# Linear attention and GEGLU block: projections, token products, later outputs and down as 64-row streams of two tiles

## The chip, the cores and the metric

The kernel runs on one core of a Trainium2 chip. The metric is the device time of one execution in microseconds (us), as a median of several runs. Inside the core, TensorE (PE) multiplies matrices into the eight banks of PSUM, each matmul with a weight load of its own (PEld); VectorE (DVE) and ScalarE (ACT) read PSUM and write SBUF; GpSimd (POOL) works on SBUF; SyncE (SP) issues most DMA transfers, plain and transposing ones, from one queue in order.

## The reference

2048 tokens of 448 features go through a layer norm, linear attention with 16 heads of 28 features, a residual, a second layer norm, a gated MLP of width 1792 and a second residual, in bfloat16.

```python
qkv = (layernorm(x) @ wqkv)            # q, k, v: 16 heads of 28
phi = lambda t: jnp.where(t > 0, t + 1, jnp.exp(t)) + 1e-6
pq, pk = phi(q), phi(k)
kv = einsum("bhsd,bhse->bhde", pk, v)
z  = einsum("bhsd->bhd", pk)
num = einsum("bhqd,bhde->bhqe", pq, kv)
den = einsum("bhqd,bhd->bhq", pq, z)[..., None] + 1e-6
h  = x + (num / den) @ wo
y  = layernorm(h)
out = h + (gelu(y @ w_gate) * (y @ w_up)) @ w_down
```

## The kernel before

The 2048 tokens are 16 tiles of 128. The program is a graph of named tasks, each on one engine; each engine runs its tasks in an order written out by hand (`ORDERS`, numbers of tasks), and waits on semaphores for what it reads. `HOLD` says of some tasks which of several waits comes first. So nothing is scheduled when it runs: an engine that waits holds back all that stands behind.

**First part, per tile.** Loads (`dx`, `dwqk`), statistics (`bnst`, `bnag`, L398, L399), logarithm and exponential for the inverse deviation on ScalarE (L405, L407), normalization on VectorE for tiles 0 to 3 (`normD`, L420) and on GpSimd for the others (`normP`, L438). The normalized tile is transposed by TensorE for tiles 0 to 3 (`tr`, L428) and by DMA for the others (`xT`, L440). Features then are the rows: 448 of them are chunks of 128, 128, 128 and 64 rows, with the last padded by zeros, so the projections to K (`k_t`) and Q (`q_t`) are four matmuls of 128 rows and 448 columns a tile (L454). ScalarE and VectorE make the positive features: for K `ek`, `ck`, `pk` (L465 to L467), for Q `eq`, `rq` (L481, L482) and later `cq`, `aq` (L533, L534). The token product (`pt`, L473) adds up normalized x times K's features over all tiles in PSUM banks 4 to 7, four matmuls a tile; chunk 3 has a row block of ones, which gives z.

**Middle.** `z1`, `z0` (L499, L500) spread z, `evp` evicts the product, `kv` (L512) multiplies it by V's weights, `kvm` (L516) masks it by heads, and `w2` (L521) folds in wo: four groups of 112 rows.

**Per pair of tiles (`a2_pair`).** `cq`, `aq`, the product with z on GpSimd (`t1`, L538), its sum per head (`dr`, L541), inverse (`rd`), the scaled features (`pn`, L545), their transposition (`tro` on TensorE for pair 0, a DMA `oT` for the others), the output (`out`, L573, four matmuls of 112 rows a tile), the residual (`hr`, L579), second statistics, normalization (`nh`), a copy `wrap` that doubles the 448 features so that gate can read them in lanes 0 to 63 and up in lanes 64 to 127, and the transposition into hnT (`trh` on TensorE for tiles 0 and 1, DMAs `hT` for the others).

**MLP.** Chunks of 2, 2, 4, 4 and 4 tiles. A group `gu` computes gate (L653) and up (L655) alternately as two 64-row streams, seven pairs for each 128 hidden features; `ge` (L673) is gelu, `hm` (L675) the product, each in two halves of 256 columns. Then `down` (L625), 14 matmuls of 128 rows a tile; `fo` (L629) adds the residual and `do` stores. w_down is loaded by `dwd`.

The decoded order of TensorE from the last projections on reads:

```
... k_14 pt1_10 pt1_11 k_15 pt1_12 q_5 pt1_13 pt1_14 pt3_10 pt1_15 pt3_11 pt3_12 pt3_13 pt3_14 pt3_15
q_7 q_6 kv q_8 w2_1 w2_3 w2_0 q_9 tro_0 w2_2 q_11 out1_0 tro_1 q_10 out1_1 q_12 q_15 q_14 out2_2
trh_0 trh_1 q_13 gu2_0 gu2_1 out2_4 gu2_2 ... gu2_9 down448_0 gu2_11 gu2_10 out2_8 down448_1 ...
```

SP's queue ends its first part with twelve `xT`, then `dwg0 dwu0 dwg1 dwu1 oT_1 oT_2 oT_3 hT_2 hT_3 dwd oT_4 ...`.

Of the kernel before, what the change touches and what calls it, by code (L numbers as in the profile page):

```python
# [740 lines left out]
```

## Time and profile before

| | |
|---|---|
| median of three runs | 193.62 us (193.48 to 193.82) |
| profiled execution, first to last instruction | 192.1 us |
| matmuls | 1572 |
| first gate/up matmul | 51.19 us from the start |
| last matmul ends | 189.7 us |
| VectorE, ScalarE, GpSimd busy | 131.0, 77.9, 50.7 us |

Times in the profile count from the first instruction. A busy time of TensorE overlaps from matmul to matmul, because the next starts before the last has left the array; what a matmul costs in a stream is therefore read from the distance of starts and not from its duration. `PE ps L454 x4` in the chain of work means four matmuls of line 454 one behind the other; "SPq" is SyncE's queue, "PEld" the weight load. A "slot" below is the distance from one matmul's start to the next one's in a full stream.

### The profile page before, as it was taken

How to read it: one execution, taken by the hardware profiler on the slowest of the kernel's cores; microseconds unless marked ns; L12 is line 12 of the kernel's file. 1: busy time of each engine (PE TensorE's matmuls, PEld its weight loads, DVE VectorE, ACT ScalarE, POOL GpSimd, SP SyncE). 2: the span in 40 equal slices, each digit the busy share in tenths (PEclk: the TensorE clock that was granted, in tenths of full speed). 3: DMA queues.
4: the chain of work that ended last, by engine and by line, in shares of the span. 5: the costliest groups of instructions: out<-in, count | busy, mean ns of one | idle time of the engine just before them, and what ended most of it. 6: DMA issues, size and time to landing. Idle time of an engine off the chain costs nothing.

```text
span 192.1 us, 4004 instructions
## 1 busy us (share of the span) xinstructions
PE 187.2 (97%) x1572; PEld 105.4 (55%) x1572; DVE 131.0 (68%) x355; ACT 77.9 (41%) x226; POOL 50.7 (26%) x92
## 2 busy tenths in 40 slices
PE   7989999999999999999999999999999999999995
PEld 7444455555778776564445545544555545455454
DVE  2899978999999998979967446736544542244412
ACT  3697745599954342043044420024444420044200
POOL 7068630560263287404190000450000000000000
PEclk9999999999999999999999999999999999999999
DMA  6976557998205977520082134307700001010011
GB/s 185 379 183 82 113 102 168 220 214 133 55 3 102 184 227 130 119 54 5 0 82 42 37 53 93 89 9 86 182 0 3 0 3 43 4 48 3 0 48 48
DMA packets 35330, 16.96 MB, mean 88 GB/s; under 512 B 27696, under 2 KB 34032, under 8 KB 35312
## 3 DMA queue, kind: packets, MB, share of 16 engines
q1 hardware_dynamic: 35168, 16.60, 41.0%
q8 instruction: 12, 0.20, 0.5%
q10 hardware_dynamic: 144, 0.11, 0.3%
q14 instruction: 6, 0.05, 0.1%
HBM read 8.26 MB, written 1.84 MB: 53 GB/s over the span
## 4 chain that ended last, share of the span: by engine, by line
PE 82%; DMA 7%; ACT 6%; DVE 3%; POOL 1%; issue 0%; SPq 0%; POOLq 0%
PE ps L653 38%; PE ps L625 22%; PE ps L454 9%; PE ps L473 6%; PE ps L573 5%; DMA wd_sb<-in_B_w_down_dram 4%; DMA x_sb<-in_A_x_dram 2%; ACT pq L482 1%; ACT eq L481 1%; DVE st L398 1%; PE ps L655 1%; DVE hh L675 1%; ACT ln L405 1%; ACT e L465 1%; DVE x_sb L579 1%; PE ps L521 0%
## 5 line engine op out<-in xcount | busy, mean ns | idle before, releaser
L653 PE MATMUL ps<-hnT,wgu_sb 64*128 64x512 bf16 (+1 forms) x490 | 86.2, 333 | 0.1
L655 PE MATMUL ps<-hnT,wgu_sb 64*128 64x512 bf16 (+1 forms) x490 | 86.3, 333 | 0.0
L673 ACT ACTIVATE gl<-ps 128x256 bf16<-128x256 f32 x112 | 37.0, 380 | 83.1 <-PE ps L653 83.0
L653 PEld LDWEIGHTS ps<-hnT,wgu_sb 64*128 64x128 bf16 x490 | 45.4, 94 | 34.5 <-issue 2.2
L675 DVE TENSOR_TENSOR hh<-ps,gl 128x256 bf16<-128x256 f32 x112 | 42.8, 417 | 30.7 <-ACT gl L673 30.6
L655 PEld LDWEIGHTS ps<-hnT,wgu_sb 64*128 64x128 bf16 x490 | 45.2, 94 | 1.2
L625 PE MATMUL ps<-wd_sb,hh 128*128 128x448 bf16 (+1 forms) x238 | 43.6, 342 | 0.2 <-DMA wd_sb<-in_B_w_down_dram 0.2
L625 PEld LDWEIGHTS ps<-wd_sb,hh 128*128 128x128 bf16 x238 | 23.0, 98 | 20.2 <-issue 0.8
L454 PE MATMUL ps<-wqk_sb,xnT 128*128 128x448 bf16 x128 | 27.9, 352 | 0.7 <-ACT xnT L433 0.6
L538 POOL TENSOR_TENSOR t<-pq,zbc 128x448 f32<-128x448 bf16 x15 | 16.6, 1117 | 38.7 <-DVE pq L534 21.9
L629 DVE TENSOR_TENSOR x_sb<-ps,x_sb 128x448 bf16<-128x448 f32 (+1 forms) x17 | 10.0, 591 | 18.3 <-PE ps L625 18.3
L398 DVE BATCH_NORM_STATS2 st<-x_sb 128x6 f32<-128x448 bf16 x32 | 19.2, 611 | 4.0 <-DMA x_sb<-in_A_x_dram 4.0
L454 PEld LDWEIGHTS ps<-wqk_sb,xnT 128*128 128x128 bf16 x128 | 12.0, 98 | 12.0 <-ACT xnT L433 0.9
L473 PE MATMUL ps<-pk,xnn 128*128 128x448 bf16 x64 | 14.1, 353 | 0.0
L573 PE MATMUL ps<-w,pqnT 112*128 112x448 bf16 x64 | 13.6, 353 | 0.0
L579 DVE TENSOR_TENSOR x_sb<-ps,x_sb 128x448 bf16<-128x448 f32 x16 | 9.7, 613 | 2.8 <-PE ps L573 2.8
L465 ACT ACTIVATE e<-ps 128x448 bf16<-128x448 f32 x16 | 8.5, 540 | 5.7 <-PE ps L454 5.7
L402 POOL TENSOR_SCALAR nm<-mv 128x1 f32<-128x1 f32 (+1 forms) x19 | 4.1, 223 | 25.2 <-DVE mv L399 24.7
L608 POOL TENSOR_SCALAR hn<-x_sb,nm,rs 128x448 bf16<-128x448 bf16 x14 | 10.5, 754 | 0.8
L545 DVE TENSOR_TENSOR pqn<-pq,rd 128x448 bf16<-128x448 bf16 x16 | 9.9, 640 | 0.0
L467 DVE SCALAR_TENSOR_TENSOR pk<-ps,e 128x448 bf16<-128x448 f32 x16 | 9.7, 614 | 0.2
L541 DVE TENSOR_REDUCE den<-t 128x16 f32<-128x448 f32 x16 | 9.7, 604 | 0.0
(65 smaller groups left out, 125.4 us busy)
## 6 DMA issues: line engine op xcount, KB each, us to landing
out_dram<-x_sb SPq DMA_DIRECT2D x15, 112.0 KB, 1.8
wd_sb<-in_B_w_down_dram SPq DMA_DIRECT2D x1, 1568.0 KB, 7.8
x_sb<-in_A_x_dram SPq DMA_DIRECT2D x3, 448.0 KB, 6.0
wgu_sb<-in_B_w_gate_dram SPq DMA_DIRECT2D x1, 896.0 KB, 12.4
wgu_sb<-in_B_w_up_dram SPq DMA_DIRECT2D x1, 896.0 KB, 16.4
wqk_sb<-in_A_wqkv_dram SPq DMA_DIRECT2D x1, 672.0 KB, 4.9
wgu_sb<-in_B_w_gate_dram SPq DMA_DIRECT2D x1, 672.0 KB, 6.2
wgu_sb<-in_B_w_up_dram SPq DMA_DIRECT2D x1, 672.0 KB, 8.7
```

What stands on the lines that cost most here:

```text
L398: op("dve", lambda e: e.bn_stats(st[:, t, :], src_ap), [b_src], [b_st[t]], "bnst%s_%d" % (tag, t))
L454: ins = e.matmul(ps[:, bk, 0:D], xnT[:, t, k, :], wqk_sb[:, k, c0:c0 + D], start=(k == 0), stop=(k == 3))
L473: ins = e.matmul(ps[:, BK_PT[c], 0:D], xnn[:, t % XN_R, c * 128:(c + 1) * 128], pk[:, ip, :], start=(t == 0), stop=(t == T - 1))
L538: op(eng, lambda e, t=t, n=n: e.tensor_tensor(t1[:, n, :], pq[:, t, :], zbc[:, :], ALU.mult), [b_pq[t]] + b_z, [b_t1[n]], "t1%s_%d" % (eng ...
L573: ins = e.matmul(ps[:, BK_OUT[n], 0:D], pqnT[0:GW, i2, n, g, :], w2[:, g, :], start=(g == 0), stop=(g == NG - 1))
L579: op("dve", lambda e, t=t, bo=bo: e.tensor_tensor(x_sb[:, t, :], ps[:, bo, 0:D], x_sb[:, t, :], ALU.add), [b_ps[bo], b_x[t]], [b_x[t]], "h ...
L608: op("pool", lambda e, t=t, sh=sh: e.tensor_scalar(hn[:, sh, 0:D], x_sb[:, t, :], nm2[:, t:t + 1], rs2[:, t:t + 1], ALU.add, ALU.mult), [b ...
L625: ins = e.matmul(psO, hh[:, j, (t % HR) * 128:(t % HR + 1) * 128], wd_sb[:, j, c0:c1], start=(j == 0), stop=(j == NJ - 1))
L653: first = e.matmul(psG[:, jj * N:(jj + 1) * N], wgu_sb[A_, k, j * 128:(j + 1) * 128], hnT[A_, ka_, c0:c0 + N], start=(k == 0), stop=(k == ...
L655: ins = e.matmul(psU[:, jj * N:(jj + 1) * N], wgu_sb[B_, k, j * 128:(j + 1) * 128], hnT[B_, kb_, c0:c0 + N], start=(k == 0), stop=(k == NK ...
L673: G.add("act", lambda e, gi=gi, cs_=cs_, psG=psG: e.activation(gl[:, gi, cs_], psG[:, cs_], AF.Gelu_apprx_tanh), r=[b_ps[BK_G[i]]], w=[b_g ...
L675: op("dve", lambda e, dst=dst, srcU=srcU, srcL=srcL: e.tensor_tensor(dst, srcU, srcL, ALU.mult), [b_ps[BK_U[i]], b_glh], [b_ar[j_][t % HR] ...
```

## The change

Two tiles are worked on together wherever TensorE can hold them as two 64-row streams, one in lanes 0 to 63 and one in lanes 64 to 127, which write different PSUM banks. Each result then takes two passes, `a` and `b`, that swap the lanes; the second pass waits on a semaphore until the first has ended (`sync`).

- Projections (`proj1`, `proj2`): tiles 0 and 1 keep four 128-row matmuls each; all other K and Q go by pairs. Pass a has chunks 0 to 2, pass b chunks 0 to 3, and in chunk 3 each tile uses its 64 rows of features alone, for which the last 64 rows of weights are loaded into both halves (`wqka`, `wqkb`).

```diff
+        def proj2(what):
+            bk0 = slot(2)
+            prev = []
+            for part, chunks in (("a", (0, 1, 2)), ("b", (0, 1, 2, 3))):
+                def fproj(e, W, part=part, chunks=chunks):
+                    ins = None
+                    for c in chunks:
+                        for i_, (kind, t) in enumerate(what):
+                            h = t % 2 if part == "b" else 1 - t % 2
+                            W(2 * c + i_)
+                            c0 = D if kind == "K" else 0
+                            ins = e.matmul(ps[:, bk0 + i_, 0:D], xnT[HALF[h], t, c, :], wqk_sb[HALF[h], c, c0:c0 + D], start=(part == "a" and c == 0), stop=(c == 3))
+                    return ins
...
+                prev = [G.add("pe", fproj, r=reads, w=[(b_ps[bk0 + i_], i_) for i_ in range(2)], name="".join("%s%d" % w for w in what) + part, mw=True, sync=prev)]
```

- Token products (`pt_pair`) run by pairs of tiles in passes of two chunks; `w2` is made by two passes of 64 and 48 rows.
- Normalized x (`xnn`) lies by pairs, an odd tile's last 64 features behind the even tile's; the odd tile needs a second small normalization (`normT`) on GpSimd. The DMA transposes of tiles 6 to 15 take a pair each (`XT_GROUPS`); xnT now lies in the space of hh.
- w2 is copied by eight small DMAs (`dw2_0` to `dw2_7`, `pack_w2`) into w2p, 448 features over 128-row chunks; pairs 2 to 7 multiply by it with 3 + 4 slots, pair 1 by w2 in rows of 64 and 48, pair 0 as before by tiles:

```diff
+                    if p < P_PACK:
+                        prog = [(g, n, KH[(s + n) % 2][0], w2) for g in range(NG) for n in range(2)]
+                    else:
+                        prog = [(g, n, HALF[(s + n + 1) % 2], w2p) for g in range(3 + s) for n in range(2)]
...
+                            ins = e.matmul(ps[:, BK_OUT[n], 0:D], pqnT[rows, i2, n, g, :], w[rows, g, :], start=(g == 0 and s == 0), stop=(g == 3 and s == 1))
```

- Down of tiles 0 to 13 runs by pairs; tiles 14 and 15 stay as they were. The residual and the store take a pair:

```diff
+        def b2_pair(a):
+            prev = []
+            for s in range(2):
+                def fnd(e, W, s=s):
+                    ins = None
+                    for j in range(NJ):
+                        for n in range(2):
+                            t, h = a + n, (s + n) % 2
+                            W(2 * j + n)
+                            ins = e.matmul(ps[:, BK_O[n], 0:D], hh[HALF[h], j, (t % HR) * 128:(t % HR + 1) * 128], wd_sb[HALF[h], j, :],
+                                           start=(s == 0 and j == 0), stop=(s == 1 and j == NJ - 1))
+                    return ins
...
+            op("dve", lambda e: e.tensor_tensor(x_sb[:, a:a + 2, :], ps[:, BK_O[0]:BK_O[1] + 1, 0:D], x_sb[:, a:a + 2, :], ALU.add),
```

- The steps `ek`, `ck`, `pk`, `eq`, `rq`, `cq`, `aq`, `dr`, `rd`, `pn`, `hr` and most `wrap` take two tiles (896 columns) in one instruction, except for tiles 0, 1, 14 and 15 where noted by `K_SINGLE` and pair 0. `ge` and `hm` take 512 columns in one instruction in the first three chunks (`WIDE = (0, 1, 2)`).
- Transposes on TensorE become 64 rows wide, two at a time, with each half evicted by another engine (`evxA`/`evxD`, `evoA`/`evoD`, `evhA`/`evhD`). For tiles 0 and 1 the copy of the normalized features is computed by GpSimd (`dupP`). `pn` of pairs 2 and later leaves a small copy on GpSimd (`pd`). The DMA transposes hT of tiles 4 and up take a pair each.
- x tiles 2 and 3 are loaded ahead of the K and Q weights:

```diff
+    LOADS = "sp:x0 act:x1 sp:x2-3 sp:wqk sp:wqka sp:wqkb sp:x4-7 sp:x8-11 sp:x12-15"
+    SEQ = "K0 Q0 K1 Q1 K2K3 Q2Q3 K4K5 K6K7 K8K9 K10K11 K12K13 K14K15 Q4Q5 Q6Q7 Q8Q9 Q10Q11 Q12Q13 Q14Q15"
```

- All orders are new. TensorE's, decoded (`pt31_2` is the pass of chunks 3 and 0, second kind, from tile 2):

```
warm tr_0 tr_1 tr_2 K0 tr_3 Q0 Q1 K1 K2K3a K2K3b pt10_0 pt10_1 Q2Q3a pt30_0 Q2Q3b pt30_1 pt11_0
pt11_1 pt31_0 K4K5a pt31_1 K4K5b pt31_2 pt11_2 pt30_2 K6K7a pt10_2 K6K7b ... K14K15a pt31_8 K14K15b
pt11_8 ... pt30_14 pt30_15 pt11_12 pt11_14 pt11_15 Q4Q5a pt10_14 pt10_15 Q4Q5b Q6Q7a kv Q6Q7b
w2a_0 w2a_2 w2b_0 Q8Q9a w2b_2 Q8Q9b tro_0 Q10Q11a tro_1 Q10Q11b out1_1 Q12Q13a out1_0 Q12Q13b
Q14Q15a trh_1 Q14Q15b outa_1 trh_0 outb_1 gu2_0 ... gu2_6 downa_0 outa_2 downb_0 outb_2 gu2_7 gu2_8
outa_3 gu2_9 outb_3 gu2_10 gu2_11 outa_4 gu2_12 gu2_13 downa_2 outb_4 downb_2 gu4_15 gu4_14 outa_5
gu4_17 gu4_16 outb_5 ... gu4_55 gu4_54 downa_12 down448_14 downb_12 down224_15 down224_15
```

VectorE's, from kvm on:

```
kvm pn1_0 dr2_2 evwD_1 pn1_1 evwD_3 evoD_0 rd2_2 cq_4 evoD_1 aq_4 pn2_2 hr1_1 bnst2_1 bnag2_1 hr1_0
nhD_1 bnst2_0 bnag2_0 dr2_4 evhD_1 nhD_0 cq_8 cq_6 aq_8 evhD_0 cq_10 aq_6 hr2_2 bnst2_3 hm0_0 dr2_6
hm0_1 bnst2_2 rd2_4 bnag2_3 hm0_2 pn2_4 hm0_3 cq_12 bnag2_2 aq_12 hm0_4 dr2_8 rd2_6 hm0_5 wrap1_2
aq_10 wrap1_3 hm0_6 ...
```

SP's: `dx0 dx2 dwqk dwqka dwqkb dx4 dx8 dx12 dwv dwv_t dwo`, seven `xT`, `dwg0 dwu0 dwg1 dwu1`, `dw2_0` to `dw2_7`, `oT_1 dwd oT_2 hT_2 hT_3 oT_3 oT_4 hT_4 hT_6 do_0 ...`.

More of the change, by code (lines that the diff above doesn't have):

```diff
@@ L77, in __init__, with add @@
         self.order = None
-    def add(self, eng, fn, r=(), w=(), name="", kind="op", after=(), mw=False, cost=(), half=()):
+    def add(self, eng, fn, r=(), w=(), name="", kind="op", after=(), mw=False, cost=(), half=(), sync=()):
         t = _Task()
@@ L96, in dep @@
             t.dep_at[d.idx] = min(t.dep_at.get(d.idx, k), k)
+        for d in sync:
+            t.deps.append(d)
+            d.ncons += 1
+            t.dep_at[d.idx] = 0
+            t.full.add(d.idx)
         r = [x if isinstance(x, tuple) else (x, 0) for x in r]
@@ new lines, in bass_sequential_preLN__linear_attn_block__glu_gated_geglu__prompt_kernel, with slot, proj1, fproj @@
+        b_xt = bufs("xt", T)
+        slots, projs = [0], []
+        def slot(n):
+            s = slots[0]
+            slots[0] = (s + n) % 4
+            return s
+        def proj1(kind, t):
+            bk = slot(1)
+            c0 = D if kind == "K" else 0
+            def fproj(e, W):
+                ins = None
+                for c in range(4):
+                    W(c)
+                    ins = e.matmul(ps[:, bk, 0:D], xnT[:, t, c, :], wqk_sb[:, c, c0:c0 + D], start=(c == 0), stop=(c == 3))
+                return ins
+            projs.append(G.add("pe", fproj, r=b_xnT[t] + [b_w[kind][0], (b_w[kind][1], 3), (b_w[kind][2], 3)], w=[b_ps[bk]], name="%s%d" % (kind, t), mw=True))
+            if kind == "K":
+                k_act(t, 1, bk)
+            else:
+                q_post(t, 1, bk)
```

486 lines of the change are left out of this document (316 added, 170 removed), and 75 rows, old and new, of tables (HOLD, ORDERS).

## The prediction

> **What bounds the kernel now.** I read the page first (busy shares, slices, the chain that ended last), then the times of stretches, then the waits, then the shapes.
>
> ```profile
> span 192.1 us, 4004 instructions
> PE 187.2 (97%) x1572; PEld 105.4 (55%) x1572; DVE 131.0 (68%) x355; ACT 77.9 (41%) x226; POOL 50.7 (26%) x92
> PEclk9999999999999999999999999999999999999999
> PE 82%; DMA 7%; ACT 6%; DVE 3%; POOL 1%; issue 0%; SPq 0%; POOLq 0%
> ```
>
> The profiled execution has 192.1 us, the median of the three runs is 193.62; the 1.5 us between them lie outside the span and I carry them over unchanged. TensorE is full, at full clock. So the first question is how many matmul slots the change takes away, the second whether the other engines let TensorE use the gap. The stretches answer where they might not (columns: length, then PE, PEld, DVE, ACT, POOL busy):
>
> ```profile
> 11.02:37.36 26.34, 26.22 (x137) 13.25 (x138) 24.04 (x68) 16.78 (x50) 13.01 (x27) 1.00 0.68 131
> 37.36:51.19 13.83, 13.70 (x100) 7.66 (x98) 13.41 (x35) 13.30 (x35) 4.90 (x5) 1.00 0.76 137
> 51.19:64.00 12.81, 12.81 (x188) 10.00 (x190) 12.51 (x37) 6.96 (x18) 5.36 (x9) 1.00 0.47 72
> 132.00:179.00 47.00, 47.00 (x393) 23.38 (x390) 20.89 (x54) 15.75 (x48) 0.00 (x0) 1.00 0.18 36
> ```
>
> Until the first gate/up group at 51.19 us VectorE is nearly as full as TensorE (13.41 of 13.83), and ScalarE too (13.30). After some 90 us only TensorE is. A slot saved late is therefore time saved; a slot saved before 51.19 counts only if VectorE's list gets shorter as well.
>
> **The price of a slot.** From the chain and from the rows of the gate/up line between 125.8 and 156.1 us:
>
> ```profile
> 26.77 3.03 PE ps L454 x16
> 50.30 0.82 ACT hnT L604
> 51.12 0.07 issue
> 51.19 0.27 PE ps L653
> 112.03 1.62 PE ps L573 x8
> 118.95 1.52 PE ps L573 x8
> 120.47 5.30 PE ps L625 x28
> 125.77 0.32 PE ps L653
> 126.09 0.21 PE ps L653
> L653 PE MATMUL ps<-hnT,wgu_sb x140: 376/376/387, 125.7 to 155.7; 64*128 64x512 bf16 x140
> L625 PE MATMUL ps<-wd_sb,hh 128*128 128x448 bf16 x210 | 40.9, 353 | 0.2 <-DMA wd_sb<-in_B_w_down_dram 0.2
> ```
>
> A 128-row matmul of 448 columns takes 3.03/16 = 0.189 us, in the down line too (5.30/28). The gate/up matmuls are 64-row streams already: 140 pairs start within 30.0 us, 30.0/139 = 0.216 us for 512 columns of both halves. That is 0.189 × 512/448: a pair of 64-row streams costs what one 128-row matmul of the same width costs. So packing for its own sake (token products, down) is worth nothing; only dropped slots count. Changing between the two forms costs time: the same eight output matmuls take 1.62 us when they come behind 64-row work and 1.52 behind 128-row work, and the first gate/up matmul behind the down line takes 0.32 instead of 0.21: 0.10 us each way.
>
> **Part by part.**
>
> *K and Q.* 448 features are 3.5 chunks of 128; before, each tile pays 4 slots. Two tiles as 64-row streams pay 3 + 4 = 7 instead of 8. Fourteen pairs: 14 × 0.189 = 2.65 us fewer, all before the gate/up groups.
>
> *Later outputs.* With w2 packed by 128 rows, pairs 2 to 7 pay 7 slots instead of 8: 6 × 0.189 = 1.13 us, all after 51.19. Pairs 0 and 1 keep 8.
>
> *Token products and down:* 64 and 196 slots as before: 0. If the pairs of 448 columns differed from 0.189 by 1 ns, the 412 slots that become such streams would move 0.4 us; I keep ±0.4.
>
> *Changes of form.* From the first gate/up group on there are 15 now (each run of L573 or L625 between gate/up groups costs two); in the new order down and outputs have the form of the groups around them, and 3 are left, at the last down tiles. 12 × 0.10 = 1.2 us saved. Before that group there is 1 now; the new order has 11 (transposes, single projections, kv, two single outputs): 1.0 us more there.
>
> *w_down.* It is moved ahead of oT_2, oT_3, hT_2 and hT_3 on SP's queue, so the wait for it goes. Nothing waits for what it now precedes: by VectorE's and GpSimd's lists oT_2 can go out only some 9 us after the first group, the load goes out before that group and lands in 7.8:
>
> ```profile
> PE ps L454 <- ACT xnT L433: 0.6, 1, 0.6
> PE ps L625 <- DMA wd_sb<-in_B_w_down_dram: 0.2, 1, 0.2
> wd_sb<-in_B_w_down_dram SPq DMA_DIRECT2D x1, 1568.0 KB, 7.8
> ```
>
> That is 0.2 us saved. The first row is the longest wait of TensorE behind its first matmul; there is little idle time to win.
>
> *Start, up to the eviction of the z rows (z1).*
>
> ```profile
> L398 DVE BATCH_NORM_STATS2 st<-x_sb 128x6 f32<-128x448 bf16 x32 | 19.2, 611 | 4.0 <-DMA x_sb<-in_A_x_dram 4.0
> 11.02 1.69 PE ps L454 x8
> ```
>
> The x tiles 2 and 3 are loaded before the projection weights, so VectorE's next statistics come in front of the normalization of tile 0, whose transposes wait about 0.5 us (one statistics step, 0.61 less its overlap); the second copy of the last K/Q weight rows adds a 112 KB load. I put the first two-tile projection at 11.4 us where the present order starts K2 at 11.02 (0.4 late). From there TensorE has 114 slots to z1 (now 121): 114 × 0.189 = 21.6. On the way K2K3b directly follows K2K3a, whose end it awaits (about 0.25, from the 0.353 us that one such matmul of L625 takes, less its slot, and a signal), and the pair-0 products wait for the second K tile's features (0.35). K4K5 needs both transposes 4 and 5 at its first matmuls, while now K4 alone starts:
>
> ```profile
> 11.90 16.48 SPq L440 DMA_TRANSPOSE xnT<-xnn  x12
> DMA to landing us min/median/max: 2.5/2.5/4.0
> L560 SPq DMA_TRANSPOSE pqnT<-pqn x7: 1232/1232/1982, 44.0 to 103.5; - x7
> DMA to landing us min/median/max: 3.0/3.1/4.9
> 34.56 0.54 ACT L499 ACTIVATE zbc<-ps 64x448 f32<-64x448 f32 x1 [0.16 <-PE ps L473]
> ```
>
> Issues follow each other at 16.48/12 = 1.37 us, so the second lands at 11.9 + 1.4 + 2.5 = 15.8, when TensorE gets there at 15.9 (21 slots and 0.6 behind 11.4); with the longest landing, 4.0, it is 1.4 us late. The first landing row is xnT's, the second pqnT's. The later pair transposes have 1024 columns, as those of pqn (median 3.1, longest 4.9); there are five instead of ten, so SP's queue is no longer full. z1 thus starts at 11.4 + 21.6 + 0.6 = 33.6, up to 35.0 with late landings; now 34.56. I take 33.7: 0.8 earlier, since 2.5 is the median.
>
> *From z1 to the first group.* Now 51.19 − 34.56 = 16.6 us. In the new order z1 to the end of kvm takes 4.75 (fixed by TensorE: 16 slots, a form change, kv's 0.82, the signal, then the 0.62 of kvm). Then comes VectorE's list up to the eviction of the second transposed tile:
>
> ```profile
> 38.88 0.82 PE ps L512 x16
> 2.44 2.01 SPq L334 DMA_DIRECT2D x_sb<-in_A_x_dram  x4
> 39.74 0.62 DVE L516 TENSOR_TENSOR kvm<-ps,mask 112x448 bf16<-112x448 f32 x1
> 42.31 1.70 DVE L545 TENSOR_TENSOR pqn<-pq,rd 128x448 bf16<-128x448 bf16 x3
> 50.47 0.62 DVE L606 COPY hnT<-ps 128x896 bf16<-128x896 bf16 x1
> 51.00 1.14 DVE L579 TENSOR_TENSOR x_sb<-ps,x_sb 128x448 bf16<-128x448 f32 x2
> L629 DVE TENSOR_TENSOR x_sb<-ps,x_sb 128x448 bf16<-128x448 f32 x15 | 9.2, 617 | 16.7 <-PE ps L625 16.7
> L629 DVE TENSOR_TENSOR x_sb<-ps,x_sb 128x224 bf16<-128x224 f32 x2 | 0.8, 392 | 1.7 <-PE ps L625 1.7
> ```
>
> A second instruction behind a first adds 0.53 us (1.14 − 0.61), and 224 more columns add 0.225, so a pair-wide step of 896 takes 0.53 + 0.47 = 1.0: joining two saves only 0.07. By that spacing the old list after kvm is 10.3 us and took 10.7 (40.36 to 51.09); the new one has more pair work in front (denominators of tiles 2 to 5, clamps and adds of tiles 6 to 9) and comes to 11.2, so about 11.7 with its waits. On SP eight small loads of w2p stand ahead of oT_1; x loads are issued at 0.5 us each, so oT_1 waits some 4 us behind the last w2 eviction, and the outputs of pair 1 come about 0.5 us late; that lies inside VectorE's list. Sum 4.75 + 11.7 + 0.2 = 16.65: no gain and no loss here, although TensorE has only some 15.5 us of work in it (68 slots, kv, the transposes of tiles 0 and 1, six form changes).
>
> *Gate/up of the first tiles.*
>
> ```profile
> L673 ACT ACTIVATE gl<-ps 128x256 bf16<-128x256 f32 x112 | 37.0, 380 | 83.1 <-PE ps L653 83.0
> L675 DVE TENSOR_TENSOR hh<-ps,gl 128x256 bf16<-128x256 f32 x112 | 42.8, 417 | 30.7 <-ACT gl L673 30.6
> ```
>
> Wide gelu and multiply (512 columns) save 0.07 us a group on VectorE. Seven groups at 1.52 us stand before the first down; VectorE's list to the seventh multiply is 12.4 us, and down needs it at 10.6 + 12 × 0.189 = 12.9: covered by half a microsecond. If that cover goes, down stalls by what is over. In chunk 2 the wide steps end 1.55 us behind a group (0.16 to leave the array, gelu 0.38 + 0.21, multiply 0.42 + 0.27 for 256 columns more each, signals) while the next-but-one needs the bank after 1.51, but an output or down pass stands between each two groups: 0.
>
> *Passes that wait for their own engine.* Each second pass waits until the first has left the array; the matmul's 0.353 less its slot leaves 0.164 us and a signal. All but K2K3b have at least one slot (0.187) of other work between, most two or more: 0.
>
> *Transposes* on TensorE become 38 pairs of 64 columns; free of cost here, from −1 (half of 56 ns each) to +2 us (twice it); those at the start show most.
>
> **Sum:** −0.8 (before the groups) − 1.13 − 1.2 − 0.2 = −3.3: span 188.8, time 190.3.
>
> **The rivals.**
>
> *A. TensorE alone decides.* Weights land so that K2K3 starts at 11.0, no transpose is late: z1 at 32.6, the first group at 49.2 (−2.0), and VectorE's waits shrink by 0.3. −2.3 − 2.5 = −4.8: 188.8. For it: TensorE hardly waits anywhere today. Against: VectorE's list of 11.2 us does not shrink.
>
> *B. Evacuation decides up to 90 us.* Late landings put z1 at 35.0, and the 51 to 90 us stretch is VectorE's (12.51 of 12.81 busy). Then half the outputs' gain (0.57) and 9 of the 12 form changes (0.9) vanish there, and 0.4 is lost before. Left: 0.57 + 0.3 + 0.2 − 0.4 = 0.7: 192.9. For it the rows of stretches; against, 2.6 us of slack that I count in VectorE's list up to the fourteenth group. [...]
>
> *C. Slower: the second passes wait visibly.* Five of them have about 0.19 us of other work between, thirteen 0.37 to 0.39. If the signal to its own engine took 0.4 us beyond the array's 0.164, they would stall 5 × 0.37 + 13 × 0.19 = 4.3, time 194.6; from a signal of 0.33 us on the gain is gone. Against: the chain has 0.07 us between the end of ScalarE's eviction (L604) and the first group that waited for it.
>
> *D. The two streams don't run side by side:* 412 slots would double, +78 us. The 140 gate/up pairs exclude it.
>
> **How the numbers follow.** Forecast 0.50, A 0.27, B 0.14, C 0.07, anything else 0.02. The time is the likeliest case's, 190.3; its own range is 189.3 to 191.4 (z1 33.4 to 34.6, ±0.4 for the slot). Eight in ten reach from A's lower side, 188.2, to just short of B, 192.5. Changes under 0.2% (0.39 us) can't be told from none. Faster: 0.50 + 0.27 + two thirds of B = 0.87; same 0.05; slower 0.08.
>
> **What would show it.** Right: 64-row matmuls of 448 columns at 0.189 a pair in the chain (0.187 would add 0.9 us of gain); the first group near 50.4 us, with TensorE idle by about a microsecond in front of it and VectorE full; no form change between 51 and 180 us; no wait for wd_sb; from the first group to the end 138.4 us instead of 140.9. Wrong: the first group at 49 (A) or 51.5 (B), idle TensorE between the gate/up groups before 80 us, or second passes that start 0.2 us late throughout (C).

## The result: 3 per cent slower, and the profile after

| | before | changed |
|---|---|---|
| median | 193.59 us (193.48 to 193.82) | 199.69 us (198.97 to 200.69) |
| ratio to before, 95% interval | | 1.0314 (1.0275 to 1.0353) |
| profiled execution | 192.1 us | 198.3 us |
| mean granted clock of TensorE in its runs | 1.000 | 0.974 to 1.000 |

The forecast was 190.3 us in a range of 188.2 to 192.5. The kernel became slower by 6.1 us, and its runs scatter by 1.7 us where those of before scatter by 0.3. The shortest of them has a granted clock of 1.000 and the longest the lowest, 0.974; but even the shortest takes 198.97 us, so the falls of the clock on record are the smaller part of the loss. In all that follows medians and ranges hold every run, while ratios leave out runs more than 1.5% above the fastest of their kernel.

The changed kernel's page: its span, the busy shares, the granted clock in 40 slices, the chain that ended last by engine.

```profile
span 198.3 us, 4730 instructions
PE 187.8 (95%) x2002; PEld 101.5 (51%) x2002; DVE 126.3 (64%) x261; ACT 71.9 (36%) x162; POOL 57.7 (29%) x105
PEclk9999999999969999999999999999999999999999
PE 79%; DVE 11%; DMA 6%; issue 1%; POOL 1%; ACT 1%; SPq 0%
```

In the chain TensorE lost 3 points, and VectorE went from 3% to 11%. One slice has a clock of 6 tenths. The loss is not spread over the kernel. The times of stretches show where it lies: first the changed kernel, then before, each cut at its own first projection behind tiles 0 and 1, at z1, at the first gate/up matmul and at the end of the last matmul, the changed kernel once more at 50.50 (columns: length, busy PE, PEld, DVE, ACT, POOL, clock, DMA share, GB/s).

```profile
0.00:14.40 14.40, 11.72 (x90) 7.14 (x92) 7.96 (x24) 6.66 (x20) 4.53 (x20) 1.00 0.81 248
14.40:37.73 23.33, 22.56 (x233) 10.57 (x234) 19.87 (x42) 11.67 (x23) 12.55 (x28) 1.00 0.62 126
37.73:50.50 12.77, 12.72 (x136) 5.98 (x132) 12.14 (x26) 10.82 (x21) 6.63 (x6) 1.00 0.82 173
50.50:58.15 7.65, 4.77 (x56) 2.05 (x54) 5.08 (x11) 4.58 (x8) 3.54 (x2) 0.78 0.78 212
58.15:195.00 136.85, 136.00 (x1500) 75.77 (x1496) 80.88 (x158) 38.16 (x92) 30.45 (x51) 1.00 0.24 49
```

```profile
11.02:34.56 23.54, 23.42 (x123) 11.79 (x124) 21.63 (x64) 16.14 (x48) 11.49 (x25) 1.00 0.63 121
34.56:51.19 16.63, 16.50 (x114) 9.12 (x113) 15.82 (x40) 13.94 (x36) 6.42 (x6) 1.00 0.82 151
51.19:189.70 138.51, 138.28 (x1266) 77.93 (x1266) 86.67 (x232) 41.77 (x126) 28.99 (x45) 1.00 0.30 59
```

So the 6.2 us come from: z1 3.2 us later (34.56 to 37.73), z1 to the first group 3.8 longer (16.63 to 58.15 − 37.73 = 20.42), the last matmul 2.4 us ahead of the end before and 3.3 now, 0.9. Against that, first group to last matmul is 1.6 shorter. All of the 3.2 us at z1 are lost ahead of the first projection of a pair (14.37 instead of 11.02); from there to z1 the changed kernel takes 23.36 us where before took 23.54. Four causes can be read off.

**The start.** The load of the K/Q weights in the list of transfers, and TensorE's instructions in order of time (start, length, line, count, in brackets the idle time ahead and who ended it), changed kernel; then the same matmuls before.

```profile
wqk_sb<-in_A_wqkv_dram SPq DMA_DIRECT2D x1, 672.0 KB, 6.5
8.31 1.67 PE L525 MATMUL ps<-wqk_sb,hh 128*128 128x448 bf16 x4 [0.56 <-DMA wqk_sb<-in_A_wqkv_dram]
10.24 4.20 PE L525 MATMUL ps<-wqk_sb,hh 128*128 128x448 bf16 x12
14.37 0.74 PE L544 MATMUL ps<-wqk_sb,hh 64*128 64x448 bf16 x6
```

```profile
6.35 0.92 PE L454 MATMUL ps<-wqk_sb,xnT 128*128 128x448 bf16 x4
7.21 2.43 PE L454 MATMUL ps<-wqk_sb,xnT 128*128 128x448 bf16 x12
```

The first K starts at 8.31 instead of 6.35, and the same twelve matmuls take 4.20 us instead of 2.43: a slot of 0.37, twice the 0.189 of the prediction. The row of granted clock shows 9 in these slices all the same; the record of the clock in the trace begins only at its first change, at 13.8 us. A slow start has to be read from the matmuls themselves.

**GpSimd's copies for tiles 0 and 1.** The two forms of normalization on GpSimd, grouped by shape (count, busy time, mean ns):

```profile
L760 POOL TENSOR_SCALAR hn<-x_sb,nm,rs 128x448 bf16<-128x448 bf16 x14 | 10.0, 718 | 0.6
...
L763 POOL TENSOR_SCALAR hn<-x_sb,mv,rs 128x448 bf16<-128x448 bf16 x2 | 3.9, 1944 | 0.2 <-ACT rs L436 0.2
```

`dupP_1` and `dupP_0` subtract the mean (mv); `nhP` adds the negated mean (nm). The first takes 1.94 us, the second 0.72.

**The queue ahead of oT_1, and the clock behind its wait.** SP's queue, then TensorE, changed kernel:

```profile
45.44 5.97 SPq L355 DMA_DIRECT2D w2p<-w  x8
51.45 1.32 SPq L708 DMA_TRANSPOSE pqnT<-pqn  x1
```

```profile
52.22 0.38 PE L777 MATMUL ps<-ident,hn 64*128 64x64 bf16 x14 [1.41 <-DVE den L675]
...
54.82 1.67 PE L737 MATMUL ps<-w,pqnT 64*128 64x448 bf16 x8 [1.47 <-DVE pq L667]
...
56.68 1.67 PE L737 MATMUL ps<-w,pqnT 64*128 64x448 bf16 x8
```

Eight small loads hold the queue for 5.97 us; oT_1, whose rows were ready at 48.1, goes out at 51.45 and lands at 54.8. The names in the brackets mislead: by the rows of the weight loads (PEld L777 and L737, waits of 1.85 and 1.91 us) the first wait ends with `dupP_1` (52.16 on GpSimd) and the second with the landing. Behind the two waits each four slots of outputs take 1.67 us (0.93 in a later run at full clock), and the clock in that stretch of 7.65 us is 0.78 on average, which is 3.4 us of half clock.

**Two smaller ones.** The waits of TensorE in total, changed kernel (total, times, longest): the third is oT_2, issued at 68.2 since its copy `pd_4` stands behind other steps on GpSimd. For the end, SP's queue: `do_6` and `do_12`, 224 KB each, go out just ahead of the last store.

```profile
PE ps L737 <- DVE pq L667: 1.5, 1, 1.5
PE ps L777 <- DVE den L675: 1.4, 1, 1.4
...
PE ps L737 <- DMA pqnT<-pqn: 0.9, 1, 0.9
PE ps L525 <- DMA wqk_sb<-in_A_wqkv_dram: 0.6, 1, 0.6
```

```profile
194.55 0.91 SPq L815 DMA_DIRECT2D out_dram<-x_sb  x2
195.52 0.55 SPq L797 DMA_DIRECT2D out_dram<-x_sb  x1
```

### The profile page after: what moved, and what is told of

Its sections match the earlier page's. It is cut to its first block, busy times and chain, and to the rows that moved or that the text cites. A ratio compares the mean times of both kernels' runs of the same rounds, so it can differ in the third digit from the quotient of the medians.

```text
span 198.3 us, 4730 instructions
## 1 busy us (share of the span) xinstructions
PE 187.8 (95%) x2002; PEld 101.5 (51%) x2002; DVE 126.3 (64%) x261; ACT 71.9 (36%) x162; POOL 57.7 (29%) x105
## 3 DMA queue, kind: packets, MB, share of 16 engines
q1 hardware_dynamic: 34528, 17.18, 38.1%
## 4 chain that ended last, share of the span: by engine, by line
PE 79%; DVE 11%; DMA 6%; issue 1%; POOL 1%; ACT 1%; SPq 0%
PE ps L858 37%; PE ps L808 17%; PE ps L737 6%; PE ps L544 5%; PE ps L579 5%; DMA wqk_sb<-in_A_wqkv_dram 3%; PE ps L525 3%; PE ps L826 3%; DVE st L427 3%; DMA pqnT<-pqn 2%; DVE hh L883 1%; DVE pk L564 1%; PE ps L856 1%; DVE e L562 1%; DVE mv L428 1%
## 5 line engine op out<-in xcount | busy, mean ns | idle before, releaser
L881 ACT ACTIVATE gl<-ps 128x256 bf16<-128x256 f32 (+1 forms) x84 | 35.2, 453 | 88.5 <-PE ps L856 86.8
L883 DVE TENSOR_TENSOR hh<-ps,gl 128x256 bf16<-128x256 f32 (+1 forms) x84 | 40.5, 507 | 39.7 <-ACT gl L881 39.7
L808 PE MATMUL ps<-wd_sb,hh 64*128 64x448 bf16 x392 | 39.5, 349 | 0.0
L808 PEld LDWEIGHTS ps<-wd_sb,hh 64*128 64x128 bf16 x392 | 19.8, 94 | 17.6 <-issue 0.4
L671 POOL TENSOR_TENSOR t<-pq,zbc 128x448 f32<-128x448 bf16 x15 | 16.7, 1129 | 26.0 <-DVE zbc L608 10.3
L544 PE MATMUL ps<-wqk_sb,hh 64*128 64x448 bf16 x196 | 22.9, 350 | 0.5 <-DVE pk L564 0.4
L579 PE MATMUL ps<-pk,xnn 64*128 64x448 bf16 x128 | 14.8, 349 | 0.3 <-DVE pk L564 0.3
L544 PEld LDWEIGHTS ps<-wqk_sb,hh 64*128 64x128 bf16 x196 | 8.7, 95 | 10.2 <-PE ps L544 1.4
L737 PE MATMUL ps<-w2p,pqnT 64*128 64x448 bf16 x84 | 9.9, 349 | 0.9 <-DMA pqnT<-pqn 0.9
L744 DVE TENSOR_TENSOR x_sb<-ps,x_sb 128x896 bf16<-128x896 f32 (+1 forms) x9 | 8.8, 982 | 2.3 <-PE ps L737 2.3
L564 DVE SCALAR_TENSOR_TENSOR pk<-ps,e 128x896 bf16<-128x896 f32 (+1 forms) x10 | 8.8, 892 | 0.1
```

Of the source, the lines that this page charges most:

```text
L544: ins = e.matmul(ps[:, bk0 + i_, 0:D], xnT[HALF[h], t, c, :], wqk_sb[HALF[h], c, c0:c0 + D], start=(part == "a" and c == 0), stop=(c == 3))
L564: op("dve", lambda e: e.scalar_tensor_tensor(pk[:, ip:ip + n, :], psK, EPS, e1[:, i:i + n, :], ALU.max, ALU.add), b_ps[bu:bu + n] + b_e1[i ...
L579: ins = e.matmul(ps[:, BK_PT[c], 0:D], xnn[HALF[h], t // 2, tcols(t, c)], pk[HALF[h], t % PK_R, :], start=(t == 0 and o == 0), stop=(t == ...
L671: op(eng, lambda e, t=t, n=n: e.tensor_tensor(t1[:, n, :], pq[:, t, :], zbc[:, :], ALU.mult), [b_pq[t]] + b_z, [b_t1[n]], "t1%s_%d" % (eng ...
L737: ins = e.matmul(ps[:, BK_OUT[n], 0:D], pqnT[rows, i2, n, g, :], w[rows, g, :], start=(g == 0 and s == 0), stop=(g == 3 and s == 1))
L808: ins = e.matmul(ps[:, BK_O[n], 0:D], hh[HALF[h], j, (t % HR) * 128:(t % HR + 1) * 128], wd_sb[HALF[h], j, :], start=(s == 0 and j == 0), ...
```

## The experiments

Theory: the two-tile streams are worth what was forecast, and the loss comes from orders, loads and one form of instruction around them, made worse by the half clock (slots of 0.37 us at the start, 3.4 us of it behind the waits of 1.41 and 1.47). Rival: steps that take two tiles at a time are too coarse, so that VectorE, ScalarE and the transposing loads set z1 and the first group.

### Keep TensorE busy at the start

```diff
+            def fill_fn(e, n_=n_):
+                for _ in range(n_):
+                    ins = e.matmul(ps[:, 3, 0:128], ones_bf[:], ones_bf[:], start=True, stop=True)
...
-warm tr_0 tr_1 tr_2 K0 tr_3
+warm fill(4) tr_0 fill(4) tr_1 fill(2) tr_2 fill(6) K0 fill(3) tr_3
```

> The changed kernel with 19 extra 128-column matmuls of ones into a spare bank of PSUM, put where TensorE is idle between 5.4 and 9 us (behind the warm-up matmuls, behind the transposes of tiles 0 to 2 and behind K0); the output does not change. Theory 'half clock at the start': the K and Q slots of tiles 0 and 1, 0.37 us each up to 14.45 us, take 0.19, K2K3 starts near 12.5 instead of 14.4, z1 moves from 37.7 to 35.7-36.3, and the time falls by 1.4 to 2.2 us to 197.5-198.3. Rival 'the tiles' normalization and the evacuation set z1, TensorE only follows': slots get shorter but z1 stays within 0.4 us of 37.7 and the time within 0.4 us of the changed kernel's.

Measured: 196.77 us (195.21 to 199.33), ratio 1.0087 (1.005 to 1.0124). TensorE's instructions of this run:

```profile
10.23 2.44 PE L606 MATMUL ps<-wqk_sb,hh 128*128 128x448 bf16 x12
12.65 1.74 PE L625 MATMUL ps<-wqk_sb,hh 64*128 64x448 bf16 x14
```

The twelve matmuls are back at 2.44 us and the first pair starts 1.7 us earlier. So the 4.20 us were the clock, and it hung here on what TensorE did just before. But z1 moved only from 37.7 to 37.0, which lies between the two expectations: a full microsecond of the gain was lost on the way. Part of the lower time came from elsewhere: TensorE waited 1.41 and 1.11 us near 50 us here too, but this profiled execution kept its full clock behind them (0.93 us for the eight output matmuls that took 1.67).

### Weights ahead of x tiles 2 and 3

```diff
-sp:x0 act:x1 sp:x2-3 sp:wqk sp:wqka sp:wqkb sp:x4-7
+sp:x0 act:x1 sp:wqk sp:wqka sp:wqkb sp:x2-3 sp:x4-7
...
-warm tr_0 tr_1 tr_2 K0 tr_3 Q0 Q1 K1 K2K3a
+warm tr_0 tr_1 K0 Q0 K1 Q1 tr_2 tr_3 K2K3a
```

> The changed kernel with the K/Q weights loaded ahead of x tiles 2 and 3, as before the change, and with the starts of three engines' orders set to that (K and Q of tiles 0 and 1 ahead of the transposes of 2 and 3). Theory 'late weights and the cold clock they bring': the weights land at 6.2-6.6 instead of 8.3, the gap in front of the first projection shrinks below 0.3 us, the clock is full from there on, z1 moves from 37.7 to 34.8-36 and the time falls by 1.7 to 3 us. Rival 'two tiles per step are too coarse for the start': the first projection is earlier but z1 stays above 37, since x2 and x3 then come later; time within 0.6 us of the changed kernel's.

Measured: 200.54 us (198.27 to 201.74); against 198.97 to 200.69 of the changed kernel no gain is shown. The weights landed at 6.7 us and K and Q of tiles 0 and 1 were done by 10.4, but then:

```profile
13.50 3.04 PE L617 MATMUL ps<-wqk_sb,hh 64*128 64x448 bf16 x14 [2.36 <-DVE pk L637]
```

The first pair waited 2.36 us for VectorE, which in my order took the statistics of tiles 2 to 5 ahead of the features of K0; the clock was half again behind that wait (14 matmuls in 3.04 us; 1.74 in the run before). z1 at 37.6. The rival's sign is right here, but the order of mine is to blame as much as pairs.

### The form of GpSimd's copy

```diff
-op("pool", ... tensor_scalar(hn[:, sh, D:2*D], x_sb[:, t, :], mv2[:, t, 0:1], rs2[:, t:t+1], ALU.subtract, ALU.mult)
+ln_negm(t, t + 1, mv2, nm2, b_mv2, b_nm2, "2")
+op("pool", ... tensor_scalar(hn[:, sh, D:2*D], x_sb[:, t, :], nm2[:, t:t+1], rs2[:, t:t+1], ALU.add, ALU.mult)
```

> The changed kernel with the duplicate features of tiles 0 and 1 made on GpSimd by adding the negated mean (one small extra instruction each) instead of subtracting the mean. Theory 'the subtract form is slow on GpSimd': each takes about 0.72 us instead of 2.00 and 1.89. Rival 'VectorE and ScalarE beside it slow it down': it stays at 1.8-2.0. In both cases the outputs of pair 1 still wait for the transposed features of oT_1 that land at 54.8, so the first gate/up group stays near 58 and the time falls by less than 0.5 us.

Measured: 199.53 us (198.61 to 200.61), ratio 1.0272 (1.0211 to 1.0333). The group of the two copies:

```profile
L837 POOL TENSOR_SCALAR hn<-x_sb,nm,rs 128x448 bf16<-128x448 bf16 x2 | 1.4, 714 | 0.8 <-POOL nm L504 0.5 <-ACT rs L509 0.3
```

0.71 instead of 1.94 us, with VectorE's list of instructions unchanged beside it (in the changed kernel it was busy for 3.54 of the 4.00 us from 50.20 on): the form is slow here, not the neighbours. (Operator and operand were changed together, so which of the two costs is not told apart.) The median hardly moves, since oT_1 is still late: TensorE waits 1.67 us for it. The first group came earlier than expected, at 56.42, because in the profiled execution the clock stayed full behind that wait (0.93 us for the eight output matmuls).

### oT_1 earlier on SP's queue

```diff
-dw2_0 ... dw2_7 oT_1 dwd
+dw2_0 dw2_1 dw2_2 dw2_3 oT_1 dw2_4 dw2_5 dw2_6 dw2_7 dwd
```

> The changed kernel with oT_1, the transposing load of pair 1, moved on SP's queue ahead of the last four of the eight small w2 loads. Theory 'SP's queue makes oT_1 late': it is issued near 49 instead of 51.45 and lands near 52.3 instead of 54.8; then the outputs of pair 1 start near 53.4 behind the K/Q work, the gap in front of them (1.47 us) goes, the clock stays full, and the first gate/up group comes 1.5 to 2.9 us earlier (58.15 to 55.3-56.6). Rival 'the slow GpSimd features set the first group': under 0.5 us gained, because transposes of tile 0 need the second slow step, that ends at 54.0, and little else is left.

Measured: 196.93 us (196.22 to 197.74), ratio 1.0137 (1.0093 to 1.0182). SP's queue:

```profile
45.09 3.52 SPq L428 DMA_DIRECT2D w2p<-w  x4
48.66 1.31 SPq L781 DMA_TRANSPOSE pqnT<-pqn  x1
```

The outputs of pair 1 start at 52.98 and take their full-clock 0.93 us instead of 1.67; the first group is at 54.94 instead of 58.15. That is 1.8 points of the ratio for one number moved in a list.

### Both together

> The changed kernel with both edits of the two runs before: duplicate features by adding the negated mean, and oT_1 issued ahead of the last four small w2 loads. Theory 'two waits one behind the other': alone the first gave the first gate/up group at 56.42 and the second at 54.94 us (58.15 in the changed kernel); together no wait over 0.5 us is left between 45 and 55 us and the group starts near 54.0, with full clock; time 195.5 to 196.3. Rival 'one of them is enough': the group stays at 54.9 and the time at 196.9, as with oT_1 alone.

Measured: 196.60 us (195.92 to 197.40), ratio 1.0129 (1.0094 to 1.0165). The first group is at 53.73: the waits were in series, as the theory says. The time did not follow: 196.9 with oT_1 alone. In the profiled execution, at 197.4 us the longest of the four, the span ends 4.6 us behind the last matmul, where it was 3.0 with oT_1 alone, and oT_2 is 1.3 us late instead of 1.1: what the first group won was given back there.

### GpSimd's copy and the store

```diff
-POOL: ... vpe2_2 negm2_2 pow2_2 pd_4 ...      SP: ... do_8 ... do_6 do_12 do_15
+POOL: ... pd_4 vpe2_2 negm2_2 pow2_2 ...      SP: ... do_6 do_8 ... do_12 do_15
```

> The changed kernel with two places in the orders moved: GpSimd's copy for pair 2 (pd_4) ahead of the variance and power steps of chunk 2, and the large store do_6 ahead of do_8. Theory 'queues': oT_2 is issued near 66 instead of 68.2, the 1.0-us wait of TensorE at 71.5 goes, and the span ends 2.4 us behind the last matmul instead of 3.3; together 1.4 to 2.0 us less than the changed kernel (197.7-198.3). Rival 'the load itself is late or VectorE is': the wait at 71.5 stays above 0.6 us, and the last store takes its 2.4 us whatever stands in front; under 0.5 us gained.

Measured: 198.50 us (195.81 to 202.18), ratio 1.0226 (1.0185 to 1.0266). The wait for oT_2 is gone; the end of the queue has one large store less, and the span ends 2.6 us behind the last matmul instead of 3.3:

```profile
PE ps L810 <- DMA pqnT<-pqn: 3.0, 1, 3.0
```

```profile
196.51 0.43 SPq L888 DMA_DIRECT2D out_dram<-x_sb  x1
197.47 0.33 SPq L870 DMA_DIRECT2D out_dram<-x_sb  x1
```

The one wait for pqnT that is left is oT_1 again: issued at 51.7 as in the changed kernel, it took 5.1 us to land instead of 3.3, TensorE idled 3.0 us, and its slots were doubled behind the wait: the eight output matmuls took 1.67 us from 56.90 on, and the first gate/up matmuls, from 60.23 to 60.87, still start 0.21 us apart (0.11 with oT_1 early). The first group is at 60.23, 2.1 us later than in the changed kernel, of which z1 accounts for 0.5; so late a landing is one source of the wide scatter. This profiled execution took 201.31 us, the second longest of the six; what the two moves are worth in time can't be read from it.

### All of these with the filled start

> All edits that cost nothing in the order of the x tiles: the extra matmuls of ones that keep TensorE busy at the start, duplicates by adding, oT_1 early, pd_4 early, do_6 early. If the losses are those named (half clock 2, first group 3.5 with its clock, oT_2 1.0, tail 0.9) and add up, the time is 191.5 to 193.5 and below the kernel of before (194.24 in the runs of this chip), with a granted clock of 1.000 in every run and little spread. If they overlap (a wait removed turns up at the next one), it stays between 194 and 196.

Measured: 193.28 us (192.72 to 193.63), ratio 0.9953 (0.9938 to 0.9968), and a granted clock of 1.000 in every run. Its stretches:

```profile
12.20:35.79 23.59, 22.79 (x233) 10.76 (x234) 20.32 (x45) 11.98 (x26) 13.54 (x29) 1.00 0.80 141
35.79:52.58 16.79, 16.05 (x188) 7.51 (x185) 16.13 (x36) 14.64 (x28) 8.11 (x9) 1.00 0.79 163
52.58:188.44 135.86, 135.86 (x1498) 113.46 (x1498) 81.94 (x160) 38.79 (x92) 30.32 (x51) 1.00 0.28 59
```

From z1 to the first group 16.79 us, from there to the last matmul 135.86 with no idle time at all, to the end of the span 138.4. What the losses named explain adds up: against the changed kernel's profile −1.9 at z1, −3.6 to the first group, −1.0 to the last matmul, −0.8 behind it, in all −7.3 (198.3 to 191.0). The medians differ by 6.4 us.

### Weights first once more, with better orders

VectorE: `bnst1_2 bnst1_3 bnag1_2 bnag1_3 ck1_0 normD_2 normD_3 pk1_0 evxD_2 evxD_3 ck1_1 pk1_1 bnst1_4 ...`; ScalarE evicts K0 at once.

> As the last one, but with the K/Q weights loaded ahead of x tiles 2 and 3, and with the orders of VectorE and ScalarE set so that nothing of tiles 0 and 1 stands behind the statistics of tiles 4 to 7: evictions of K0 first, its features next. Theory 'late weights': the first two-tile projection starts at 11.3-12.0 us instead of 12.65 and z1 at 35.5-36.3 instead of 37.0; 0.5 to 1.2 us below the kernel of the last run. Rival 'statistics, normalization and feature steps of the pairs set z1': z1 stays at 36.7-37.3 and the time within 0.4 us of the last run's.

Measured: 194.72 us (193.51 to 195.22), ratio 1.0018 (0.9995 to 1.004). TensorE:

```profile
10.82 0.35 PE L625 MATMUL ps<-wqk_sb,hh 64*128 64x448 bf16 x1 [0.45 <-DVE hh L575]
11.97 1.71 PE L625 MATMUL ps<-wqk_sb,hh 64*128 64x448 bf16 x13 [0.80 <-ACT eq L668]
...
17.45 0.36 PE L625 MATMUL ps<-wqk_sb,hh 64*128 64x448 bf16 x1 [0.29 <-DVE pk L645]
18.03 0.74 PE L625 MATMUL ps<-wqk_sb,hh 64*128 64x448 bf16 x5 [0.22 <-DMA hh<-xnn]
```

The first pair starts 1.4 us earlier than in the last run, and z1 comes at 36.5, 0.7 later. The rival's case: K4K5 starts at 17.45 and goes on at 18.03, as late as in the last run (17.52). There the transposing load of tile 4 landed slowly (4.4 us); here it is issued 1.2 us later, since the statistics of tiles 4 and 5 stand behind the features.

### Statistics of tiles 4 and 5 as early as before

VectorE: `... bnag1_3 bnst1_4 normD_2 normD_3 ck1_0 bnst1_5 bnag1_4 bnag1_5 evxD_2 evxD_3 pk1_0 ck1_1 pk1_1 ...`; ScalarE: `eq1_0 rq1_0` ahead of `evxA_2`.

> As the run with the weights first, with one difference in the orders: VectorE takes the statistics of tiles 4 and 5 as soon as they land (about 8.2 us), ahead of the features of K0 and K1, as in the kernel before, and ScalarE evicts Q0 ahead of the transposes of tiles 2 and 3. Theory 'the supply of normalized tiles sets z1': the transposing load of tile 4 is issued near 12.3 instead of 14.17, TensorE's waits between 10 and 18 us shrink from 3.2 to 1.5 us or less, z1 comes at 35.0-35.5 instead of 36.46 and the time is 192.0-192.9. Rival 'the list of VectorE as a whole sets it': what the statistics win the features lose, z1 stays at 36.2 or later and the time at 194 or more.

Measured: 192.81 us (192.69 to 192.97), ratio 0.9919 (0.9888 to 0.995). This is the fastest version, 1.4 us below the runs of before on the same chip (194.20). TensorE:

```profile
11.76 1.74 PE L625 MATMUL ps<-wqk_sb,hh 64*128 64x448 bf16 x14 [1.24 <-DVE pk L645]
...
17.44 0.74 PE L625 MATMUL ps<-wqk_sb,hh 64*128 64x448 bf16 x6 [1.25 <-DVE pk L645]
```

The transposed tile 5 is there at 16.7, but K4K5 still starts at 17.44: now the bank holds it, until `pk2_2`, the third of three pair-wide steps, ends at 17.39. The time is what the theory said, z1 at 35.9 is between the two expectations. TensorE's waits of this run (total, times, longest):

```profile
PE ps L625 <- DVE pk L645: 2.5, 2, 1.2
...
PE ps L660 <- DVE pk L645: 0.3, 1, 0.3
```

The first row is the two waits just shown. From 17.44 us to z1 TensorE waits 0.3 us in all: what the waits for pairs cost in this run is lost before 17.5 us, and from there on TensorE's own work sets z1.

### The load order alone, in the kernel before

```diff
         dma_x("sp", 0, 1)
         tx1 = dma_x("act", 1, 2)
+        dma_x("sp", 2, 4)
         dma_w3("sp", wqk_sb, 0, 2 * D, b_wqk, "dwqk")
         dma_w1("sp", wqk_sb, 0, 2 * D, b_wqk, "dwqk_t")
-        dma_x("sp", 2, 4)
```

> The kernel before, with nothing changed but that x tiles 2 and 3 are loaded ahead of the K/Q weights, as the change has it (without the extra weight rows). Theory 'this order of loads costs the start': the weights land at 7.8-8.3 us instead of 6.18, TensorE idles from 6 us on, its clock falls to half until 11-14 us, z1 moves from 34.56 to 36.3-37.2, and the time rises by 1.6 to 2.8 us. Rival, as the prediction had it: the first K2 is 0.4 us later at most, and the time rises by less than 0.5 us.

Measured: 197.75 us (196.76 to 197.85), ratio 1.0161 (1.0122 to 1.0201). TensorE, and the eviction of z1:

```profile
8.83 0.94 PE L466 MATMUL ps<-wqk_sb,xnT 128*128 128x448 bf16 x4 [2.42 <-DMA wqk_sb<-in_A_wqkv_dram]
...
9.72 4.12 PE L466 MATMUL ps<-wqk_sb,xnT 128*128 128x448 bf16 x12
```

```profile
L511 ACT ACTIVATE zbc<-ps x1: 539/539/539, 37.9 to 37.9; 64x448 f32<-64x448 f32 x1
```

One line moved, in a kernel of single tiles, and z1 goes from 34.6 to 37.9 and the time up by 1.6%, 3.1 us. The weights land 2.6 us later (8.8 instead of 6.2) though only 224 KB more are in front of them, and the twelve matmuls take 4.12 us. That is as much as the changed kernel loses up to z1 (3.2), without any pairs. It is more than I expected.

### Fewer warm-up matmuls, in the kernel before

```diff
-    WARM = 40
+    WARM = 16
```

> The kernel before with 16 instead of 40 warm-up matmuls of ones, so that TensorE idles from about 3 to 5.5 us; the loads and all orders stay. Theory 'the clock is granted only behind a few full microseconds of TensorE': the first K and Q slots take 0.37 us, up to 10-13 us, z1 moves to 35.5-36.5 and the time rises by 0.8 to 2 us. Rival 'the clock at the start does not hang on what TensorE did': slots of 0.19 us from the first on and a time within 0.3 us of before.

Measured: 195.41 us (194.67 to 196.44), ratio 1.0062 (1.0037 to 1.0086).

```profile
6.23 1.65 PE L466 MATMUL ps<-wqk_sb,xnT 128*128 128x448 bf16 x4
...
7.89 3.09 PE L466 MATMUL ps<-wqk_sb,xnT 128*128 128x448 bf16 x12
```

Only the idle time ahead of the first transposes differs, 2.3 us, and the slots are 0.37 us up to 9.2 us, with z1 at 35.3 (0.7 later). So the clock hung on how busy TensorE was just before, here (3.09 us for the twelve matmuls instead of 2.43) as in the filled start (2.44 instead of 4.20). How long TensorE has to be busy for the full clock, or idle for the half, no run shows: it idled for 2.3 us here, and ahead of the half clock behind 54.8 us in the changed kernel for 1.41 and 1.47, with work between. The loss is 0.6% of the time here.

### Pull the first pair's feature steps together

VectorE: `... bnst1_9 ck2_2 pk2_2 bnst1_8 ...`; ScalarE: `ek2_2` ahead of `ln1_6`.

> The kernel of the run with the statistics of tiles 4 and 5 first, with the three pair-wide feature steps of K2K3 pulled together: ScalarE's eviction ek2_2 ahead of the root of tiles 6 and 7, VectorE's ck2_2 and pk2_2 ahead of the statistics of tile 8 and the sums of 9. There K4K5 waited 1.25 us for pk2_2, that ended at 17.39, while its transposed features had landed at 16.72. Theory 'the pair-wide chain of eviction, clamp and add (0.90 + 0.97 + 1.09 us) holds the PSUM banks of K': pk2_2 ends at 16.4-16.6, K4K5 starts at 16.7-16.9 instead of 17.44, z1 comes at 35.2-35.4 instead of 35.87 and the time is 0.4 to 0.7 us below that run's, 192.1-192.5. Rival 'VectorE's list as a whole': K4K5 starts earlier, but K6K7 or K8K9 wait instead, z1 stays at 35.7 or later and the time within 0.2 us of 192.8.

Measured: 193.19 us (192.86 to 194.59), ratio 0.9973 (0.9956 to 0.9989).

```profile
16.82 0.74 PE L625 MATMUL ps<-wqk_sb,hh 64*128 64x448 bf16 x5 [0.15 <-DMA hh<-xnn]
...
20.51 0.74 PE L625 MATMUL ps<-wqk_sb,hh 64*128 64x448 bf16 x6 [0.82 <-DMA hh<-xnn]
```

K4K5 is free at 16.82 and K6K7 waits 0.82 us instead, because the statistics that were pushed back delay its transposing load. z1 at 36.2 is the rival's result; the time is 0.4 us above the last version's, measured on another chip, and so no gain either.

### All runs side by side

| run | median | ratio to before, 95% interval | z1 | first gate/up | span |
|---|---|---|---|---|---|
| before | 193.59 | | 34.6 | 51.19 | 192.1 |
| changed | 199.69 | 1.0314 (1.0275 to 1.0353) | 37.7 | 58.15 | 198.3 |
| filled start | 196.77 | 1.0087 (1.005 to 1.0124) | 37.0 | 55.52 | 195.0 |
| weights first | 200.54 | not given | 37.6 | 57.40 | 197.9 |
| copy by adding | 199.53 | 1.0272 (1.0211 to 1.0333) | 38.1 | 56.42 | 196.9 |
| oT_1 early | 196.93 | 1.0137 (1.0093 to 1.0182) | 37.4 | 54.94 | 195.1 |
| both | 196.60 | 1.0129 (1.0094 to 1.0165) | 36.9 | 53.73 | 195.7 |
| pd_4, do_6 | 198.50 | 1.0226 (1.0185 to 1.0266) | 38.3 | 60.23 | 199.6 |
| all, filled start | 193.28 | 0.9953 (0.9938 to 0.9968) | 35.8 | 52.58 | 191.0 |
| all, weights first | 194.72 | 1.0018 (0.9995 to 1.004) | 36.5 | 53.26 | 191.8 |
| all, statistics early | 192.81 | 0.9919 (0.9888 to 0.995) | 35.9 | 52.69 | 191.1 |
| before, x2 and x3 first | 197.75 | 1.0161 (1.0122 to 1.0201) | 37.9 | 54.49 | 196.1 |
| before, 16 warm-ups | 195.41 | 1.0062 (1.0037 to 1.0086) | 35.3 | 51.89 | 193.4 |
| all, pair chain | 193.19 | 0.9973 (0.9956 to 0.9989) | 36.2 | 53.05 | 191.5 |

Each ratio is against runs of before on the same chip, whose medians were 193.59 to 194.24.

## Why the prediction was wrong

**Right: the slot, the outputs, the form changes, w_down, second passes.** A pass of three slots takes 0.57 us (13.71 to 14.28 in the run with the statistics early), 0.19 a slot. From the first group to the end of the span the prediction said 138.4 us instead of 140.9; with the wait for oT_2 and the late store taken away it is 138.4. No engine waits for wd_sb, and of the second passes only K2K3b, which follows its first pass directly, visibly waits, for the 0.25 us that it was priced at (its 14 matmuls take 1.74 us, 14 others in two passes that do not depend on each other 1.50): rivals C and D fall. Before those two were taken away the stretch was 140.2: the changed kernel kept 0.7 of 2.5 us. No run takes the outputs, the form changes and w_down apart, so of the 2.5 us only the sum is shown.

**Wrong: "0.4 late", the start.** The step priced the new load order by VectorE's next statistics alone, and put the later landing of the weights at nothing, without a reason. They land at 8.3 instead of 6.2, and TensorE, idle in between for 0.17 to 0.56 us at a time, gets its slots at 0.37: the first pair starts at 14.37, not 11.4. The run with that order alone in the old kernel loses 3.3 us at z1, as much as the changed kernel. Repairing the start does not win all of it back, though, because of the next step.

**Wrong: "114 slots to z1", the way of the pairs.** 22.3 us were forecast from the first pair to z1; it took 23.4 in the changed kernel, and 23.6 to 25.6 in the four versions in which the clock never fell. Part of this was wrong in the sum from the start: by the same count the 121 slots of before are 22.9 us, and its row has 23.54. In the changed kernel TensorE waited 0.7 us on this way, so there the form of the sum held and its size was off by 1.1. But with an earlier first pair the waits grow: wherever the first matmul of K2K3 stood between 10.8 and 12.2 us, K4K5 got going only between 16.8 and 18.0, K6K7 between 20.15 and 20.96, and z1 stayed at 35.8 to 36.5. Up to there that is the mechanism of rival B (z1 at 35.0): the three pair-wide feature steps hold the banks of K for 0.90 + 0.97 + 1.09 us, and the statistics between them feed the transposing loads of the next pair; moving one delayed the other. From K6K7 on TensorE takes 15.2 to 15.7 us to z1 in these versions and in the changed kernel alike. Of the 2.65 us of slots saved in K and Q nothing reaches the first gate/up group: it comes at 52.58 at the earliest, 51.19 before.

**Wrong: "no gain and no loss here", z1 to the first group.** 16.65 was forecast, 20.42 came. Two things were late that the sum put at nothing. The eight loads of w2p were taken at 0.5 us each behind the last w2 eviction, and what that delays as covered by VectorE's list; they took 5.97. And `dupP` has no term in the sum, though its operands have a form that costs 1.94 us. The two idle stretches then cost more than themselves, because the clock fell to half for 3.4 us. With the waits gone the stretch is 16.8, the forecast number, but that is in part luck: TensorE is busy for 16.05 of it, not 15.5, and its one wait left is for GpSimd's copy and not for VectorE:

```profile
PE ps L859 <- POOL hn L845: 0.6, 1, 0.6
```

**Not in the prediction: the clock.** The page of before says full clock everywhere, and I took that as a property of the kernel. It was the property of a TensorE that never idled for more than 0.6 us behind its first matmuls: with 2.3 us of idle time at the start the same kernel ran at half clock there. Which wait brings half clock is not settled by its length alone: 1.41 + 1.47 us did in the changed kernel, 1.41 + 1.11 in the filled start and two of 1.25 in the fastest version did not. None of the rivals had the clock, so the one that ended slower (C) had the wrong place, and the range excluded 199.7. The small losses behind the last matmul (0.9) and at oT_2 (0.9) were order effects that the sum did not look for.

The chances gave slower 0.08. What was missing was not a finer sum over slots but a look at each queue that the change reorders: SP's at the start, SP's before oT_1, GpSimd's before the first transposes.

**What stays open.** Which link of the chain from statistics to transposing load is the first to shorten was not settled. A version with the K steps of one tile each (`K_SINGLE`), which would test directly whether their joining holds up the start, was not run. Transposing tiles 4 and 5 on TensorE, as tiles 0 to 3 are, wasn't tried, because its PSUM banks are in use by the token products then.

## What to carry to other kernels

A saved matmul slot is worth its time only where TensorE stays fed; price a change's new orders queue by queue (who issues, what stands ahead, when it lands) before its slots. On a kernel whose TensorE is always busy, an idle stretch can cost more than its length: here waits of 1.41 and 1.47 us came ahead of 3.4 us at half clock, an estimated 1.7 us of work lost on top (half of the 3.4), while behind two waits of 1.25 us in the fastest version the clock was full. Where tiles are joined in pairs, look at how long the pair holds its banks and at who makes the next pair's input, not only at the sum of the joined steps.
